# First eight attention steps without normalized weights: 1/sum is turned by TensorE and applied to the values

## The chip, the cores and the metric

The kernel runs on one core of a Trainium2 chip. The metric is the device time of one execution in microseconds; the kernel before was timed three times and the median counts. A core has five engines that each work through their own queue in program order: TensorE (PE) for matrix products and transposes, VectorE (DVE), ScalarE (ACT), GpSimd (POOL) and SyncE (SP), whose queue here issues nearly all DMAs. An instruction waits for semaphores that other instructions raise, and everything behind it on its engine waits with it.

## The reference

Attention over 8 sequences of 576 tokens with 8 heads of 64, in which only weights close to the largest survive, then an MLP with an ELU. All is float32.

```python
scores = scale * np.matmul(q, k.transpose(0, 1, 3, 2))
thresh = np.max(scores, axis=-1, keepdims=True) - tau
scores = np.where(scores >= thresh, scores, -1000000000.0)
scores = scores - np.max(scores, axis=-1, keepdims=True)
attn = np.exp(scores)
attn = attn / (np.sum(attn, axis=-1, keepdims=True) + 1e-09)
return np.matmul(attn, v).astype(np.float32)
...
h = x @ w_in
g = np.where(h > 0.0, h, alpha * (np.exp(np.minimum(h, 0.0)) - 1.0))
return (g @ w_out).astype(np.float32)
```

The division by the row's sum can be done on the weights, before the product with v, or on the product, since the sum belongs to a row of queries.

## The kernel before

Heads are taken two at a time: a pair `pr` is one sequence's heads 2j and 2j+1, four pairs to a sequence. A pair has five steps `i`: four blocks of 128 queries, and one (`NC`) with the last 64 queries of both heads. `steps` (L1175, L1176) lists them; for the first sequence the order is (0,0), (0,1), (1,0), (1,1), (2,0), (2,1), (3,0), (3,1), and then steps 2, 3 and NC of each pair. The numbers 0 to 7 in the task names are these first eight steps, and they make the first half (`part` 0, 256 queries) of the values of pairs 0 to 3.

A step goes through these functions, each an instruction or a few:

- `scores` (L657): PE forms 128 x 576 scores for each of the two heads in PSUM.
- `max_of` (L728, DVE), `bound_of` (L732, POOL) or `pivot_of` (L742, DVE): the row's largest score and the threshold.
- `exp_of` and `mask_of` (L761, L771): ACT makes the exponential, DVE keeps those above the threshold and adds up the row. Or `sink_of` and `raise_of` (L750, L756), where ACT does both. `mask_of` reads the scores in PSUM and frees their banks for a later step's `scores`.
- `total_of` (L778) and `reciprocal_of` (L785): DVE forms the sum and, at L789, its reciprocal `rs`, 128 x 2: one number for each query and head.
- a normalization for each head, which multiplies 128 x 576 weights by `rs`: on POOL (`normalize`, L722, instruction at L726), DVE (`normalize_dve`, L706, L709) or ACT (`normalize_act`, L711, L714). Which, is listed by hand in `ACT_NORM` and `NORM_DVE`; POOL has the rest.
- `turn_parts` (L803): PE turns the weights, 128 x 128 at a time (`transpose`, L791), into `rt` in PSUM, and ACT or DVE copies them into `wTa` or `wTb` (L808).
- `values` (L915): when a part's steps are turned, PE multiplies with v, one product with `vd` (L925) and eight with `vm` (L930), into `pv` in PSUM.
- `values_out` (L1055): ACT copies `pv` into `xt`, the MLP's input (L1060).

In the early phase `rt` and `pv` share two PSUM buffers. `room_for` keeps a queue of them: whoever wants a third first lets the oldest be read out.

The order of the instructions on all engines in this phase is made by `early_tasks` (L1308). Each `task` has a due time, a correction by hand from the table `MOVED`, and the tasks that it needs. The tasks are taken by due time, and `do` (L1299) first does what a task needs. A task that nothing pulls forward stands where its due time puts it; a large due time means that it is done just when something needs it. So the due times fix a program order and nothing else; on the chip an instruction runs when it is at the head of its queue and its semaphores are up.

Around the change:

- The queries of pair 0 come in two pieces. The first 256 are loaded at the start. The rest are loaded by `load_rest_of_q` (L1337) into the buffer `qr`, 128 x 320, of which there is one, and turned by DVE in `rest_of_q` (L1342); they are needed from the ninth step, (0,2), on.
- SP issues loads in program order (L544 for q and k, L558 and L560 for v, L478 for pieces of the MLP's weights, `wst`). In the stretch that matters here, the order is: k and q of a later pair, the four DMAs of `qr`, one `wst`, v of pair 3, v of pair 2, then more `wst`. v of a pair is two `vm` and two `vd`.
- The weights of the MLP come in a form that POOL, ACT and DVE convert between the attention's instructions (`convert_rest` L485, `convert_shift` L492 and L494, `convert_add` L500, `convert_rest_pool` L505, `convert_abs` L510, `convert_end` L518).
- The MLP's first product, `ffn1` (L1091, PE at L1102), starts when all four pairs' `xt` exist.

Of the kernel before, what the change touches and what calls it, by code (L numbers as in the profile page):

```python
# [10 lines left out]
FP32 = mybir.dt.float32  # L11
# [4 lines left out]
ALU = mybir.AluOpType  # L16
# [352 lines left out]
def kernel(  # L369
# [10 lines left out]
    nc = tc.nc  # L380
    PSUM = bass.MemoryType.PSUM
    P = 128
    B, H, S, D = q.shape
# [5 lines left out]
    T = 32  # L389
    NT = P // T  # L390
# [3 lines left out]
    NPAIR = H // 2  # L394
# [22 lines left out]
    wstage = early.enter_context(tc.tile_pool(name="wstage", bufs=2))  # L417
    wpool = [wstage]
    banks = ExitStack()
    psum = {"t": banks.enter_context(tc.tile_pool(name="ps_t", bufs=2, space=PSUM))}  # L420
# [214 lines left out]
    wTs, xts, open_steps, turns = {}, {}, {}, {}  # L635
# [142 lines left out]
    def total_of(pr, i, hs):  # L778
        st = open_steps[pr, i]
        cs = slice(hs[0], hs[-1] + 1)  # L780
        if "summed" not in st:
            st["summed"] = True
            nc.vector.tensor_reduce(st["su"][:, cs], st["sm"][:, cs], axis=AX.X, op=ALU.add)

    def reciprocal_of(pr, i, hs):  # L785
        st = open_steps[pr, i]
        cs = slice(hs[0], hs[-1] + 1)
        total_of(pr, i, hs)
        nc.vector.reciprocal(st["rs"][:, cs], st["su"][:, cs])  # L789

    def transpose(dst, src):  # L791
        nc.tensor.matmul(dst, src, idents[-1], is_transpose=True, skip_group_check=True)  # L792
# [104 lines left out]
    def fetch(pr, i):  # L897
        back = turns.pop((pr, i)).rearrange("c k p n -> (c k) p n")
        wT, g0 = turned_tile(pr, i)
        if i < NC:  # L900
            nc.sync.dma_start(wT[:, g0 : g0 + NT].rearrange("p g c n -> p g (c n)"), back)
        elif pr >= JOINED:
            for h in range(2):
                g = h * (3 * NT - 2)
                nc.sync.dma_start(
                    wT[:, g : g + 2, h * NC : h * NC + NC + 1].rearrange("p g c n -> p g (c n)"),
                    back[:, 2 * h : 2 * h + 2],
                )
        else:
            nc.sync.dma_start(  # L910
                wT.rearrange("p (a b) c n -> p a b (c n)", b=2)[:, ::5],
                back.rearrange("k (a b) n -> k a b n", b=2),
            )

    def values(pr, part, pv=None):  # L915
        b, j = divmod(pr, NPAIR)
# [138 lines left out]
    def values_out(pr, part, pv):  # L1055
        b, j = divmod(pr, NPAIR)
        q0, n = TAIL * part, (3 if part else 2) * NT * T
        watch = on_banks if wide else lambda *a: None
        o = pv[:, q0 : q0 + 2 * P]
        watch(nc.scalar.copy(xts[b][:, j, part * 2 * P : (part + 1) * 2 * P], o), o)  # L1060
        if part:
            xs = opool.tile([P, TAIL], FP32, name="xs", bufs=2)
            for h in range(2):
                r = slice(h * D, (h + 1) * D)
                o = pv[r, h * (n - TAIL) : h * (n - TAIL) + TAIL]
                watch(nc.scalar.copy(xs[r], o), o)  # L1066
            nc.sync.dma_start(xtail[j, :, b * TAIL : (b + 1) * TAIL], xs)
            pairs.pop(pr), raws.pop(pr)
# [106 lines left out]
    steps = [(pr, i) for pr in range(NP) for i in ((0, 1, NC, 2, 3) if pr >= JOINED else range(NB))]  # L1175
    steps[:per_seq] = [(pr, i) for x in ((0, 1), (2, 3, NC)) for pr in range(NPAIR) for i in x]  # L1176
    LATE = 10

    def behind(pr, i):
        if i in (1, NB - 1):  # L1180
# [114 lines left out]
    def task(x, t, key, f, *needed):  # L1295
        each = "_".join(map(str, x)) if isinstance(x, tuple) else x
        made[x] = [t + (MOVED.get(key, 0.0) if key else 0.0) + MOVED.get(each, 0.0), len(made), f, needed, False]

    def do(x):  # L1299
        job = made[x]  # L1300
        if not job[4]:
            job[4] = True
            for y in job[3]:
                if y:
                    do(y)
            job[2]()

    def early_tasks():  # L1308
# [5 lines left out]
        def room_for(pool, release):  # L1314
            while len(taken[pool]) >= 2:
                taken[pool].popleft()()
            taken[pool].append(release)
# [54 lines left out]
        for pr in range(1, NPAIR + 6):  # L1372
            old = ("sc", number[pr - 2, NC]) if pr > 1 else None
            own = pr < NPAIR
            for x, name in enumerate("qk"):
                n = 2 * pr - 2 + x if own else number[pr - 1, 2 + x]
                k, late_ = kind(n), n >= LATE
# [26 lines left out]
                m = number[pr, 2] if own and not x else n  # L1404
# [15 lines left out]
        for i, (n, x) in enumerate(slots):  # L1420
            late_, k, t = n >= LATE, f"{kind(n)}{x}", begin[n]
            m, y = slots[max(i - 4, 0)]
# [47 lines left out]
        for n in range(MIDDLE):  # L1470
            pr, i = steps[n]
# [4 lines left out]
            t, k, hs, late_ = begin[n], kind(n), heads_of(i), n >= LATE  # L1476
# [10 lines left out]
            for h in hs:  # L1487
                task(("max", n, h), at_(0.2 + 0.5 * h, 1.8 + 0.6 * h, 0.8 + 0.5 * h), f"max{h}{k}", lambda pr=pr, i=i, h=h: max_of(pr, i, h), ("sc", n))
                back = ("turned", n - (2 if last_ else WBUFS)) if n >= WBUFS else None
                t_exp, t_th, t_mask = (at_(0.3 + 0.7 * h, 2.0 + 0.6 * h, 1.0 + 0.5 * h), at_(0.4 + 0.7 * h, 2.2 + 0.6 * h, 1.1 + 0.5 * h),  # L1490
                                       at_(2.0 + 1.6 * h, 5.6 + 0.1 * h, 4.0 + 0.1 * h))
                if (n, h) in MASK_ACT:
                    task(("exp", n, h), t_exp, f"exp{h}{k}", lambda pr=pr, i=i, h=h: sink_of(pr, i, h), ("th", n, h), back, "late" if last_ else None)
                    task(("th", n, h), t_th, f"th{h}{k}", lambda pr=pr, i=i, h=h: pivot_of(pr, i, h), ("max", n, h))
                    task(("mask", n, h), t_mask, f"mask{h}{k}", lambda pr=pr, i=i, h=h: raise_of(pr, i, h), ("exp", n, h))
                else:
                    task(("exp", n, h), t_exp, f"exp{h}{k}", lambda pr=pr, i=i, h=h: exp_of(pr, i, h),
                         ("max", n, h), exps[-1] if exps else None, ("mask", *exps[-2][1:]) if len(exps) > 1 else None)
                    task(("th", n, h), t_th, f"th{h}{k}", lambda pr=pr, i=i, h=h: bound_of(pr, i, h), ("max", n, h))
                    exps.append(("exp", n, h))  # L1500
                    task(("mask", n, h), t_mask, f"mask{h}{k}", lambda pr=pr, i=i, h=h: mask_of(pr, i, h), ("exp", n, h), ("th", n, h),
                         ("mask", n, 0) if h and (n, 0) not in MASK_ACT else back, "late" if last_ else None)
                scaled = normalize_act if (n, h) in ACT_NORM else normalize_dve if (n, h) in NORM_DVE else normalize_pool
                norm = lambda pr=pr, i=i, h=h, f=scaled: f(pr, i, h)
                task(("norm", n, h), at_(5.0 + 0.8 * h, 6.2 + 0.1 * h, 5.4 + 0.1 * h), f"norm{h}{k}", norm, ("rec", n))
            task(("su", n), at_(3.8, 5.8, 4.4), f"su{k}", lambda pr=pr, i=i, hs=hs, f=total_act if n in SU_ACT else total_of: f(pr, i, hs), *[("mask", n, h) for h in hs])
            task(("rec", n), at_(3.8, 5.8, 4.4), f"rec{k}", lambda pr=pr, i=i, hs=hs: reciprocal_of(pr, i, hs), ("su", n))
            norms, part = [("norm", n, h) for h in hs], int(i >= 2)
# [9 lines left out]
            else:  # L1518
# [11 lines left out]
                m = n + 1  # L1530
# [14 lines left out]
            if i in (1, NC) and n < MIDDLE - 4:  # L1545
                got = []
                mine_ = [number[pr, x] for x in ((0, 1) if i == 1 else (2, 3, NC))]

                def run_values(pr=pr, part=part, got=got):
                    room_for("t", lambda: do(("out", pr, part)))  # L1550
                    got.append(values(pr, part))

                def run_out(pr=pr, part=part, got=got):
                    got[0]()
                    if (pr, part) == (NPAIR - 1, 0):
                        push_ffn(0)
                    elif (pr, part) == (NPAIR - 1, 1):
                        push_ffn(1)

                m = n + 2  # L1560
                t_val, t_out = (begin[m] + 4.0, begin[m] + 6.2) if m < LATE else (begin[m] + 0.4, begin[m] + 3.3)
                if n < per_seq:
                    t_val, t_out = begin[n + 1] + 4.2, begin[n + 2] + 1.5
                    if n >= LATE:
                        t_val, t_out = begin[n + 1] + 5.6, begin[n + 1] + 6.8
                elif any(m in SQUARES for m in mine_):
                    t_val, t_out = begin[n + 3] + 5.7, begin[n + 3] + 5.8
                elif SWITCH + 1 >= m >= SWITCH:
                    t_val, t_out = t_val - 8.0, t_out - 8.0
                task(("val", pr, part), t_val, f"val{k}", run_values, *[("landed", m) for m in mine_], ("v", pr))  # L1570
                task(("out", pr, part), t_out, f"out{k}", run_out, ("val", pr, part), ("out", pr, 0) if part else None)
            if n == 0:
                task("idle", t + 2.1, None, lambda: idle(16))
            if n >= SWITCH:
# [40 lines left out]
    with tc.manual_schedule():  # L1615
# [471 lines left out]
        for pr in range(JOINED, NP + 2):  # L2087
            t = clock[0]
# [263 lines left out]
```

## Time and profile before

| | us |
|---|---|
| median of three runs | 1258.88 (1258.06 to 1259.68) |
| profiled execution | 1259.32 |
| its span, first to last instruction | 1257.5 |
| PE busy | 1243.9 |
| DVE busy | 1040.3 |
| POOL busy | 727.1 |
| ACT busy | 635.2 |

A row of the time line has start, duration, engine, source line, operation, output and input with the tile's size, the number of instructions that it merges, and in brackets how long the engine was idle before and what ended that. "SPq" is SyncE's queue issuing a DMA. A row of the chain of waits has start, length, and the engine, tile and line. A row of groups has line, engine, operation, names, shapes and count, then busy us and the mean ns of one, then idle time ahead of the group. The table by stretches lists for each stretch the busy us and, in brackets, the instructions of each engine, then the granted clock and the DMA share.

### The profile page before, as it was taken

Reading aid. Unit: us, or ns where it says so; the run is one execution under the profiler, and the core shown is the slowest. Engines: PE = TensorE matmul, PEld = TensorE weight load, DVE = VectorE, ACT = ScalarE, POOL = GpSimd, SP = SyncE. Lnnn points to the kernel's source line nnn. Section 1 sums busy time; section 2 is a strip of 40 time slices with the busy share of each in tenths; the row PEclk is TensorE's granted clock in tenths of the full one; section 3 lists DMA queues with packets and bytes.
Section 4 is the critical chain, followed back from the end, with each engine's and each line's share of the span. In section 5 each row is a group of like instructions: output and inputs, shape, how many; then the busy total and the mean of one; then the engine's idle time right before and its main releaser. Section 6 shows DMA issues by size and latency. Waiting matters only on the chain.

```text
span 1257.5 us, 21116 instructions
## 1 busy us (share of the span) xinstructions
PE 1243.9 (99%) x6598; PEld 957.0 (76%) x6598; DVE 1040.3 (83%) x2199; ACT 635.2 (51%) x1331; POOL 727.1 (58%) x1061
## 2 busy tenths in 40 slices
PE   8999999999999999999999999999999999999998
PEld 6676576467878787888778787878788887788886
DVE  7888778789798988898889879898889876776983
ACT  7989776664352526253534435252625353465330
POOL 4778655687475847666576747584766655122000
PEclk9999999999999999999999999999999999999999
DMA  7557688998889898998989998999889885000001
GB/s 134 151 177 177 177 244 234 260 248 216 239 239 266 245 240 224 241 263 228 252 206 253 237 231 231 256 257 240 228 238 262 221 241 175 20 1 1 1 34 34
DMA packets 325551, 245.74 MB, mean 195 GB/s; under 512 B 209216, under 2 KB 289984, under 8 KB 325440
## 3 DMA queue, kind: packets, MB, share of 16 engines
q1 hardware_dynamic: 323264, 243.65, 72.2%
q8 instruction: 52, 0.85, 0.3%
q10 hardware_dynamic: 2176, 0.75, 0.2%
q14 instruction: 59, 0.48, 0.1%
HBM read 154.53 MB, written 89.78 MB: 194 GB/s over the span
## 4 chain that ended last, share of the span: by engine, by line
PE 90%; DVE 3%; DMA 2%; ACT 2%; issue 1%; SPq 1%; POOL 1%; DVEq 0%; ACTq 0%; POOLq 0%
PE f L1678 23%; PE f L1818 22%; PE sc L977 8%; PE sc L1050 7%; PE f L2278 7%; PE f L2203 5%; PE f L1102 4%; PE sc L673 3%; PE f L1154 3%; PE f L2216 2%; PE pv L930 2%; PE rt L792 1%; PE sc L1042 1%; PE sc L1037 1%; DMA there<-x 1%
## 5 line engine op out<-in xcount | busy, mean ns | idle before, releaser
L984 DVE TENSOR_REDUCE mx<-sc 128x1 f32<-128x576 f32 x207 | 148.3, 750 | 28.5 <-PE sc L977 24.6
L726 POOL TENSOR_SCALAR w<-w,rs 128x576 f32<-128x576 f32 x144 | 115.8, 813 | 70.0 <-DVE rs L789 69.8
L1004 ACT ACTIVATE w<-sc,mx 128x576 f32<-128x576 f32 x113 | 81.5, 740 | 116.0 <-DVE mx L984 98.7
L868 DVE STREAM_TRANSPOSE x<-w 128x512 f32<-128x512 f32 (+1 forms) x153 | 108.9, 744 | 15.3 <-POOL w L726 11.3
L996 POOL TENSOR_SCALAR th<-mx,ntau 128x2 f32<-128x2 f32 (+1 forms) x114 | 33.8, 297 | 133.3 <-DVE mx L984 133.3
L977 PE MATMUL sc<-kT,qT 64*128 64x448 f32 (+4 forms) x736 | 103.4, 416 | 0.2 <-ACT xs L1066 0.2
L977 PEld LDWEIGHTS sc<-kT,qT 64*128 64x128 f32 x736 | 81.0, 186 | 25.1 <-issue 16.5
L1011 DVE SCALAR_TENSOR_TENSOR w<-sc,th,w 128x576 f32<-128x576 f32 x113 | 88.2, 811 | 9.4 <-ACT w L1004 9.2
L1678 PE MATMUL f<-xt,sw 128*128 128x256 f32 x384 | 93.8, 386 | 1.8 <-DVE g L1700 1.8
L1678 PE MATMUL f<-xt,w_in 128*128 128x256 f32 x384 | 92.2, 382 | 0.0
L1818 PE MATMUL f<-w_out,s 128*128 128x256 f32 x384 | 92.0, 382 | 0.1
L1818 PE MATMUL f<-w_out,g 128*128 128x256 f32 x384 | 92.0, 382 | 0.0
L1678 PE MATMUL f<-x,w_in 128*128 128x256 f32 x384 | 90.9, 379 | 0.0
L1818 PE MATMUL f<-t,s 128*128 128x256 f32 x384 | 90.8, 379 | 0.0
L726 POOL TENSOR_SCALAR e<-e,rs 128x576 f32<-128x576 f32 x91 | 67.1, 741 | 35.6 <-DVE rs L789 34.2
L1678 PEld LDWEIGHTS f<-xt,sw 128*128 128x128 f32 x384 | 69.4, 189 | 18.6 <-issue 4.8
L1678 PEld LDWEIGHTS f<-xt,w_in 128*128 128x128 f32 x384 | 71.7, 190 | 12.7 <-ACT w L1692 2.2
L1818 PEld LDWEIGHTS f<-w_out,g 128*128 128x128 f32 x384 | 72.0, 190 | 12.4 <-issue 3.1
L1818 PEld LDWEIGHTS f<-w_out,s 128*128 128x128 f32 x384 | 71.9, 190 | 12.4 <-issue 2.5
L1678 PEld LDWEIGHTS f<-x,w_in 128*128 128x128 f32 x384 | 72.8, 190 | 10.5 <-ACT s L1692 0.6
L1818 PEld LDWEIGHTS f<-t,s 128*128 128x128 f32 x384 | 72.8, 190 | 10.3 <-POOL s L1765 0.4
L1765 POOL TENSOR_TENSOR s<-g 128x256 f32<-128x256 f32 x96 | 74.9, 785 | 7.9 <-DVE g L1728 7.5
(316 smaller groups left out, 3103.5 us busy)
## 6 DMA issues: line engine op xcount, KB each, us to landing
there<-x SPq DMA_DIRECT2D x444, 144.0 KB, 3.5
wTb<-there SPq DMA_DIRECT2D x58, 576.0 KB, 6.5
wTa<-there SPq DMA_DIRECT2D x53, 576.0 KB, 5.0
sw<-win_sums SPq DMA_DIRECT2D x46, 384.0 KB, 4.9
t<-wout_sums SPq DMA_DIRECT2D x33, 512.0 KB, 6.2
qm<-in_q_dram SPq DMA_DIRECT2D x124, 72.0 KB, 4.9
wst<-in_moe_w_in_dram SPq DMA_DIRECT2D x16, 512.0 KB, 4.4
vm<-in_v_dram SPq DMA_DIRECT2D x64, 128.0 KB, 3.9
```

The source lines that it names most:

```text
L726: nc.gpsimd.tensor_scalar(wv, wv, st["rs"][:, h : h + 1], 1.0, ALU.mult, ALU.mult)
L868: nc.vector.transpose(x[:, :, c0 : c0 + nc_], src.rearrange("p (c g n) -> p g c n", c=nc_, n=T))
L977: on_banks(nc.tensor.matmul(o, qT[r, i * P : (i + 1) * P], kT[r, k0 : k0 + n], start=True, stop=True, skip_group_check=True), o)
L984: on_banks(nc.vector.tensor_reduce(st["mx"][:, h : h + 1], st["sc", h], axis=AX.XY if i == NC else AX.X, op=ALU.max, negate=True), st["sc" ...
L1004: on_banks(nc.scalar.activation(st["e", h], st["sc", h], AF.Exp, bias=st["mx"][:, h : h + 1]), st["sc", h])
L1011: on_banks(nc.vector.scalar_tensor_tensor(st["e", h], st["sc", h], st["th"][:, h : h + 1], st["e", h], ALU.is_ge, ALU.mult, accum_out=st[" ...
L1050: on_banks(nc.tensor.matmul(o, vm[:, h, c], parts[part][:, g0:g1, h * (NC + 1) + c], start=False, stop=(c == NC - 1), skip_group_check=Tru ...
L1678: nc.tensor.matmul(loc["banks"][place], left[:, j], right[:, j], start=(begins and j == 0), stop=(j == 1), skip_group_check=True)
L1765: engine.tensor_tensor(o, x, y, op)
L1818: nc.tensor.matmul(place(m), lhs, rhs, start=(begins and v == 0), stop=(v == RU - 1), skip_group_check=True)
L2203: nc.tensor.matmul(o, w.rearrange("p (j f) -> p j f", j=KJ)[:, j], m, start=(j == 0 and x == 0), stop=(j == KJ - 1 and x == 1), skip_group ...
L2278: nc.tensor.matmul(banks8[2 * i + x // 2], h[:, tok], w, start=(f == 0 and x != 1), stop=(f == NFT - 1 and x != 0), skip_group_check=True)
```

## The change

Part 0 of pairs 0 to 3 is `UNSCALED`: `(0,0)`, `(1,0)`, `(2,0)`, `(3,0)` as (pair, part).

- The normalizations of the first eight steps (16 in all) are not done.
- For these steps the reciprocal writes 128 x 128 instead of 128 x 2: each head's number is written 64 times beside itself, into one of three buffers `rsd`.
- Ahead of the values of such a part, PE turns the two steps' `rsd` into one `rt` buffer (`spread`): row h*64+d, column query holds 1/sum of that query for head h, which is the layout of `pv`.
- ACT copies these 256 columns into SBUF (`keep_spread`). The room for this is the buffer `qr`, the same one that the rest of pair 0's queries is loaded into.
- DVE multiplies `pv` by it into `xt`, in place of ACT's copy.
- The new tasks have a due time of 9000, so they stand right before the first that needs them. In program order the kept scales of pairs 0 and 1 come before the load of `qr`, those of pairs 2 and 3 behind its use.

```diff
+        if (pr, int(i >= 2)) in UNSCALED:
+            st["rs"] = wstage.tile([P, 2, D], FP32, name="rsd", bufs=3)
+            nc.vector.reciprocal(st["rs"], st["su"].unsqueeze(2).broadcast_to([P, 2, D]))
+            return
         nc.vector.reciprocal(st["rs"][:, cs], st["su"][:, cs])
...
+    scales = {}
+
+    def spread(pr):
+        rt = psum["t"].tile([P, 512], FP32, name="rt", tag="rt")
+        for i in range(2):
+            transpose(rt[:, i * P : (i + 1) * P], open_steps[pr, i]["rs"].rearrange("p h d -> p (h d)"))
+        return rt
+
+    def keep_spread(pr, rt):
+        room = wstage.tile([P, S // T - 2 * NT, T], FP32, name="qr", bufs=1).rearrange("p j d -> p (j d)")
+        scales[pr] = room[:, : 2 * P]
+        nc.scalar.copy(scales[pr], rt[:, : 2 * P])
...
-        watch(nc.scalar.copy(xts[b][:, j, part * 2 * P : (part + 1) * 2 * P], o), o)
+        if (pr, part) in UNSCALED:
+            nc.vector.tensor_tensor(xts[b][:, j, : 2 * P], o, scales.pop(pr), ALU.mult)
+        else:
+            watch(nc.scalar.copy(xts[b][:, j, part * 2 * P : (part + 1) * 2 * P], o), o)
...
+    UNSCALED, LAST = [(pr, 0) for pr in range(NPAIR)], 9000.0
...
+                if (pr, int(i >= 2)) in UNSCALED:
+                    norm = lambda: None
...
+                    def run_spread(pr=pr, got_spread=got_spread):
+                        room_for("t", lambda: do(("scales", pr)))
+                        got_spread.append(spread(pr))
+
+                    task(("spread", pr), LAST, None, run_spread, *[("rec", m) for m in mine_])
+                    task(("scales", pr), LAST, None, lambda pr=pr, got_spread=got_spread: keep_spread(pr, got_spread[0]),
+                         ("spread", pr), ("out", pr - 1, 0) if pr else None)
-                task(("val", pr, part), t_val, f"val{k}", run_values, *[("landed", m) for m in mine_], ("v", pr))
-                task(("out", pr, part), t_out, f"out{k}", run_out, ("val", pr, part), ("out", pr, 0) if part else None)
+                task(("val", pr, part), t_val, f"val{k}", run_values, *[("landed", m) for m in mine_], ("v", pr),
+                     ("spread", pr) if (pr, part) in UNSCALED else None)
+                task(("out", pr, part), t_out, f"out{k}", run_out, ("val", pr, part),
+                     ("out", pr, 0) if part else ("scales", pr) if (pr, 0) in UNSCALED else None)
```

On the queues this gives: on SP the same DMAs in the same order, but the first of `qr` now waits until DVE's multiplication for pair 1 has read the buffer. On DVE that multiplication stands right behind a `convert_end` (L518) of the seventh step; the multiplication for pair 3 stands between the `pivot_of` (L748) and the `convert_shift` (L494) and `mask_of` (L775) of the tenth step. On PE the two transposes of `rsd` stand right ahead of each part's values.

More of the change, by code (lines that the diff above doesn't have):

```diff
@@ L1569, in early_tasks @@
                     t_val, t_out = t_val - 8.0, t_out - 8.0
-                task(("val", pr, part), t_val, f"val{k}", run_values, *[("landed", m) for m in mine_], ("v", pr))
-                task(("out", pr, part), t_out, f"out{k}", run_out, ("val", pr, part), ("out", pr, 0) if part else None)
+                if (pr, part) in UNSCALED:
+                    got_spread = []
+                    def run_spread(pr=pr, got_spread=got_spread):
[8 more added lines that the diff above has]
+                     ("out", pr, 0) if part else ("scales", pr) if (pr, 0) in UNSCALED else None)
             if n == 0:
```

## The prediction, as it was put on record

> **What bounds the kernel now.** The page's head and the table by stretches come first.
>
> ```profile
> span 1257.5 us, 21116 instructions
> PE 1243.9 (99%) x6598; PEld 957.0 (76%) x6598; DVE 1040.3 (83%) x2199; ACT 635.2 (51%) x1331; POOL 727.1 (58%) x1061
> ...
> 0.00:62.40 62.40, 55.80 (x344) 40.04 (x344) 47.95 (x113) 50.61 (x98) 38.60 (x70) 1.00 0.62 143
> 62.40:1257.50 1195.10, 1188.11 (x6254) 916.95 (x6254) 992.34 (x2087) 584.60 (x1234) 688.49 (x992) 1.00 0.73 198
> ...
> 12.00:36.00 24.00, 21.66 (x147) 14.45 (x145) 20.54 (x48) 21.48 (x42) 15.62 (x27) 1.00 0.81 169
> ...
> 37.90:62.40 24.50, 23.41 (x143) 16.89 (x141) 20.01 (x44) 22.72 (x45) 19.78 (x26) 1.00 0.42 132
> ```
>
> The columns behind the comma are PE, PEld, DVE, ACT and POOL. From 62.4 us on PE is idle for 1195.1 - 1188.1 = 7.0 us in all, so whatever the first 62 us gain or lose reaches the end nearly whole. The change touches only those, and there no engine is full. What sets the pace there stands in the chain of waits:
>
> ```profile
> 12.63 1.33 POOL w L726 x2
> ...
> 14.07 0.75 POOL x L584
> ...
> 28.30 0.53 DVE w L709
> ...
> 37.98 0.63 PE pv L925 x2
> 38.60 1.88 PE pv L930 x16
> 40.48 1.32 PE sc L673 x8
> ...
> 62.41 0.41 PE rt L792 x2
> ```
>
> Two things are to be seen. Of the sixteen normalizations that go, only those at 12.63 and 28.30 are on the chain. And pair 2's values (37.98, 38.60) are on it: who delays them delays the run.
>
> **The change part by part.**
>
> *Gain.* At 12.63, 1.33 us leave the chain, but its next link, POOL's scaling at 14.07, needs queries that DVE turns until 12.47 + 0.78 = 13.25; so I take 14.07 - 13.25 = 0.8 of it. At 28.30 all 0.53 leaves. Together 1.3 us, and 1.9 at most. The others ran beside other work.
>
> ```profile
> 12.47 0.78 DVE L577 STREAM_TRANSPOSE x<-qm 128x576 f32<-128x576 f32 x1
> ```
>
> *Reciprocals.* The trace has no wide one. Its nearest rows:
>
> ```profile
> L789 DVE RECIPROCAL rs<-su 128x2 f32<-128x2 f32 x128 | 21.1, 165 | 10.0 <-ACT su L720 6.1
> ...
> L789 DVE RECIPROCAL rs<-su 128x1 f32<-128x1 f32 x32 | 5.2, 163 | 3.7 <-ACT su L720 2.8
> ...
> L808 DVE COPY wTb<-rt 128x128 f32<-128x128 f32 x4 | 1.1, 272 | 0.0
> ...
> L1700 DVE TENSOR_TENSOR g<-f,t 128x256 f32<-128x256 f32 x48 | 20.3, 422 | 1.6
> ```
>
> The second element costs 2 ns, so 128 come to 163 + 127 x 2 = 417 ns; a copy of as many takes 272. Between these I take 0.36 us, 0.19 over the narrow form. Six of them (steps 0 to 5) stand ahead of the place that decides: 1.2 us of DVE work (0.6 to 1.5). A multiplication of 128 x 256 is priced like the product out of PSUM in the last row, 0.42. So DVE has 1.2 + 0.42 - 0.53 = 1.1 us more to do up to there, against a gain of 1.3 on the chain: even. I keep early DVE times as they are, with 1.3 us to either side.
>
> *The load of `qr`.* This is the main term. It must now wait for pair 1's multiplication, and SP issues in order.
>
> ```profile
> 27.21 2.00 SPq L544 DMA_DIRECT2D qr<-in_q_dram  x4
> 29.26 0.46 SPq L478 DMA_DIRECT2D wst<-in_moe_w_in_dram  x1
> ...
> 33.18 0.59 SPq L558 DMA_DIRECT2D vm<-in_v_dram  x1
> 33.81 0.51 SPq L560 DMA_DIRECT2D vd<-in_v_dram  x1
> ```
> ```profile
> vd<-in_v_dram SPq DMA_DIRECT2D x1, 16.0 KB, 2.5
> ```
> ```profile
> 35.03 0.69 DVE L518 SCALAR_TENSOR_TENSOR w_in<-wtop,wst 128x512 f32<-128x512 f32 x1
> ...
> 37.29 0.51 DVE L1342 STREAM_TRANSPOSE x<-qr 128x320 f32<-128x320 f32 x1
> ```
> ```profile
> 29.95 1.95 PE L930 MATMUL pv<-wTb,vm 128*64 128x256 f32 x16
> ...
> 37.91 0.70 PE L925 MATMUL pv<-wTa,vd 128*128 128x256 f32 x2
> ```
>
> The multiplication stands behind L518, which ends at 35.03 + 0.69 = 35.7; it ends at 36.1, and `qr`, issued at 27.21 before, goes out at 36.2: 9.0 us late. Queued behind it are one `wst`, the v of pair 3 and the v of pair 2. The last `vd` of pair 2 was issued at 33.81 and took 2.5 us to land, 36.3; pair 2's values began at 37.91, so 1.6 us were spare. Now it lands at 36.3 + 9.0 = 45.3 and the values begin at 45.4: 7.5 us late (6.2 to 8.8). PE works in order, so all its later work stands behind.
>
> Two other engines are held by the same load. DVE's turning of `qr` at 37.29 waits till about 36.2 + 2.0 + 1.9 = 40.1, and ACT's conversion of the late `wst` (37.06 below) till it has landed, 29.26 + 4.4 + 9.0 = 42.7 at the soonest:
>
> ```profile
> qr<-in_q_dram SPq DMA_DIRECT2D x1, 40.0 KB, 1.9
> ...
> wst<-in_moe_w_in_dram SPq DMA_DIRECT2D x1, 512.0 KB, 4.4
> ```
> ```profile
> 37.06 0.68 ACT L510 ACTIVATE wst<-wst 128x512 int32<-128x512 f32 x1
> ```
>
> Both are shorter than 7.5 us and lie under it, but they leave neither engine free to run ahead. Where the stall goes: it isn't taken up again, as between 37.9 and 62.4 PE had only 24.5 - 23.4 = 1.1 us idle.
>
> *Pair 3's multiplication.* It is put ahead of L494 and L775 on DVE and waits for the values:
>
> ```profile
> 47.92 1.95 PE L930 MATMUL pv<-wTb,vm 128*64 128x256 f32 x16
> ...
> 50.44 1.21 PE L673 MATMUL sc<-x,qd 128*128 128x288 f32 x4
> ```
> ```profile
> 48.95 0.42 DVE L494 TENSOR_SCALAR wtop<-wst 128x512 uint32<-128x512 uint32 x1
> 49.46 0.82 DVE L775 SCALAR_TENSOR_TENSOR w<-sc,th,e 128x576 f32<-128x576 f32 x1
> ```
>
> In the times of before: the values end at 47.92 + 1.95 = 49.87, two transposes later 50.1; the multiplication ends at 50.5, L494 at 50.9, and the mask starts 1.4 us behind 49.46. The scores of 50.44 wait for that mask's PSUM banks. I take 1.0 us (0.5 to 1.5), as PE's wait at 62.4 gives some back.
>
> *The remaining edits cost nothing.* The first six transposes of `rsd` run while PE waits for v or for ACT; uncovered they would be a tenth of a microsecond each. ACT's copies of the scales take the place of its copies of `pv`, of the same size.
>
> *PE's clock.* While it waits for v, PE stands still for 45.4 - 38.1, some 7 us. What does it run at then?
>
> ```profile
> 1.48 4.66 PE L792 MATMUL rt<-ident 128*128 128x128 f32 x22 [1.48 <-POOL ident masks.py:199]
> ...
> 9.56 1.23 PE L673 MATMUL sc<-x 64*128 64x288 f32 x4 [1.12 <-ACT w L753]
> 10.72 1.97 PE L792 MATMUL rt<-ident 128*128 128x128 f32 x16
> ```
>
> The first 22 transposes took 0.21 us each, 16 later ones 0.12, these soon after a pause of 1.12 us. No row has a pause of 7 us. If it works like a start, pair 2's values (37.91 to 40.4, 2.5 us) take 0.21/0.12 as long, 1.9 us more; if like the short pause, nothing. A pause that long is nearer to the start; since some of the stretch waits for other engines anyway I take 1.4.
>
> [...]
>
> *Sum.* 7.5 + 1.0 + 1.4 = 9.9 us, to the profiled execution's own 1259.32, which is 0.44 above the median: 1269.2, or 1268.8 beside the median. Ends: 6.2 + 0.5 + 0 = 6.7 and 8.8 + 1.5 + 1.9 = 12.2, so 1265.6 to 1271.1.
>
> **The rivals.**
>
> *Each element of a reciprocal costs what the first does.* A small operation on one element beside it:
>
> ```profile
> L436 DVE TENSOR_SCALAR keep<-pos 128x1 f32<-128x1 f32 x1 | 0.2, 154 | 0.1
> ```
>
> The reciprocal of one element takes 163 - 154 = 9 ns more. If each of 128 pays about that, one takes 0.154 + 128 x 0.009 = 1.3 us, 1.14 more than before; six are 6.8 us ahead of pair 1's multiplication. DVE was idle for 24.0 - 20.5 = 3.5 us between 12 and 36, which takes up part, not all, since the chains behind grow as well: 4.8 us on the end, 1273.6. Against it: the second element costs 2 ns. For it: two elements are few, and a floor under small sizes would hide it. [...]
>
> *The delay is partly taken up.* If ACT, POOL and DVE, rid of sixteen normalizations, run ahead behind 42 us, PE makes up its 1.1 us of idle time, and the early end holds: 6.2 - 1.1, 1264.0. Against it: of the normalizations still on the chain there, none goes.
>
> *Not slower.* If the multiplication for pair 1 is over by 27.21 + 1.6 = 28.8, pair 2's v comes in time, and what is left is the gain: 1258.9 - 1.3 = 1257.6. That is the point that decides. Against it: the multiplication needs pair 1's values, which end at 29.95 + 1.95 = 31.9, and no normalization of 1.3 us moves these by more than 3 us.
>
> **How the numbers follow.** The forecast as put, 1265.6 to 1271.1: 0.52. Slow reciprocals: 0.34. Partly taken up: 0.10. Not slower: 0.04, of which 0.03 is faster. Changes below 0.2% (2.5 us) can't be told from none here. The predicted time is that of the forecast, 1268.8. The range goes from 1264 to 1275, the one end for the delay partly taken up, the other for slow reciprocals with all their other terms at full. Faster 0.03, within 0.2% 0.02, slower 0.95.
>
> **What would show it.** SP's issue of `qr` at about 36 instead of 27 us, with its wait named for DVE; PE's row of pair 2's first product at about 45, idle some 7 us before it and released by a DMA of v; the transposes or products right behind at nearly twice their time; the mean of the wide reciprocal, under 0.45 us or over 1; the stretch from pair 3's values to the first MLP products about 1 us longer. If `qr` goes out before 30 us, the main term falls; if it does go late and pair 2's values don't start late, the order of the v loads was read wrongly.

## The result, and the profile after

The changed kernel takes 1272.26 us (median of four runs, 1271.29 to 1273.45); beside it the kernel before took 1258.47. The ratio is 1.0108, 95% interval 1.0095 to 1.0121: 13.6 us slower by the ratio, 13.8 by the two medians. The forecast was 1268.8. The profiled execution took 1271.29, with a span of 1269.5, 12.0 longer than before; it is the shortest of its four, and that of before lay above its median, so the spans show less than the medians.

The head of the page of after, and the table by stretches (columns as before), first for before from its first MLP product on, then for after:

```profile
span 1269.5 us, 21115 instructions
...
PE 1247.2 (98%) x6606; PEld 958.4 (75%) x6606; DVE 1047.3 (83%) x2202; ACT 633.0 (50%) x1327; POOL 720.0 (57%) x1050
```
```profile
51.48:1257.50 1206.02, 1198.52 (x6313) 925.41 (x6311) 1002.23 (x2104) 594.61 (x1254) 697.88 (x1002) 1.00 0.73 198
```
```profile
64.51:1269.50 1204.99, 1198.46 (x6313) 925.25 (x6311) 1002.32 (x2104) 593.80 (x1252) 699.04 (x1002) 1.00 0.73 198
40.00:45.00 5.00, 0.43 (x4) 0.19 (x2) 2.99 (x6) 0.00 (x0) 0.07 (x1) 0.91 0.83 199
45.00:50.00 5.00, 2.66 (x10) 1.48 (x12) 0.98 (x3) 3.60 (x7) 3.11 (x4) 0.50 0.83 234
50.00:55.00 5.00, 5.00 (x36) 3.17 (x34) 2.59 (x6) 1.61 (x3) 0.66 (x1) 0.91 0.05 20
```

From the first MLP product on PE was idle for 1206.02 - 1198.52 = 7.5 us before and is for 1204.99 - 1198.46 = 6.5 us after, with the same 6313 instructions and the same busy time. So of the 13.0 us by which that product comes late, 1.0 is made up behind it, and 12.0 reach the end. Most of the loss lies in one hole, 40 to 50 us, where PE did 3.1 us of work in 10; from 45 to 50 us PE had a granted clock of 0.50.

The time line of after, SP's queue, then PE, then DVE, then POOL and ACT:

```profile
38.10 1.82 SPq L544 DMA_DIRECT2D qr<-in_q_dram  x4
...
44.81 0.47 SPq L560 DMA_DIRECT2D vd<-in_v_dram  x1
```
```profile
39.99 0.44 PE L796 MATMUL rt<-ident,rsd 128*128 128x128 f32 x2
47.34 1.19 PE L942 MATMUL pv<-wTa,vd 128*128 128x256 f32 x2 [6.91 <-ACT e L768]
48.46 3.14 PE L947 MATMUL pv<-wTa,vm 128*64 128x256 f32 x16
...
59.22 0.62 PE L942 MATMUL pv<-wTb,vd 128*128 128x256 f32 x2
...
63.47 1.21 PE L673 MATMUL sc<-x,qd 128*128 128x288 f32 x4 [1.17 <-DVE w L775]
64.51 1.89 PE L1122 MATMUL f<-xt,w_in 128*128 128x256 f32 x8
```
```profile
37.62 0.42 DVE L1078 TENSOR_TENSOR xt<-pv,qr 128x256 f32<-128x256 f32 x1
...
41.59 0.51 DVE L1363 STREAM_TRANSPOSE x<-qr 128x320 f32<-128x320 f32 x1 [2.08 <-DMA qr<-in_q_dram]
...
54.98 0.94 DVE L791 RECIPROCAL rsd<-su 128x128 f32<-128x128 f32 x1
...
61.83 0.42 DVE L1078 TENSOR_TENSOR xt<-pv,qr 128x256 f32<-128x256 f32 x1 [0.94 <-PE pv L947]
62.17 0.42 DVE L494 TENSOR_SCALAR wtop<-wst 128x512 uint32<-128x512 uint32 x1
62.50 0.81 DVE L775 SCALAR_TENSOR_TENSOR w<-sc,th,e 128x576 f32<-128x576 f32 x1
```
```profile
44.93 1.04 POOL L492 TENSOR_TENSOR wtop<-wst,eight 128x512 int32<-128x512 int32 x1 [7.09 <-DMA wst<-in_moe_w_in_dram]
```
```profile
47.19 0.73 ACT L753 ACTIVATE w<-sc,th 128x576 f32<-128x576 f32 x1
```

What SP's queue waited for (total us, times, longest), and the groups of the two new operations:

```profile
SPq L544 <- DVE xt L1078: 9.8, 1, 9.8
```
```profile
L791 DVE RECIPROCAL rsd<-su 128x128 f32<-128x128 f32 x8 | 7.6, 952 | 0.6 <-ACT su L720 0.4
L1078 DVE TENSOR_TENSOR xt<-pv,qr 128x256 f32<-128x256 f32 x4 | 1.7, 421 | 3.6 <-PE pv L947 3.6
```

Pair 1's multiplication ends at 38.04 and SP, which stood 9.8 us for it, issues `qr` at 38.10. The last `vd` of pair 2 goes out at 44.81 and takes 2.4 us to land in this trace, so it is there at 47.2; pair 2's values start at 47.34. The row names ACT's exponential as the releaser, but that only happened to end at nearly the same moment, 46.56 + 0.72 = 47.28. With v loaded first (below) the same product starts 6 us ahead of that exponential. In the run with 44 transposes v comes later: there the exponential ends at 47.51, the last `vd` goes out at 46.05, and the product starts at 48.56, again 2.5 us behind the `vd`, and names it.

The shift against before, place by place: pair 2's values start 47.34 - 37.91 = 9.4 late, pair 3's 59.22 - 47.29 = 11.9, the scores behind them 63.47 - 50.44 = 13.0, the first MLP product 64.51 - 51.48 = 13.0. And a wide reciprocal took 0.95 us, not 0.36.

### The profile page after: what moved, and what is told of

Same layout as the page of the kernel before. It is cut to its first block, busy times and chain, and to the rows that moved or that the text cites. A ratio compares the mean times of both kernels' runs of the same rounds, so it can differ in the third digit from the quotient of the medians.

```text
span 1269.5 us, 21115 instructions
## 1 busy us (share of the span) xinstructions
PE 1247.2 (98%) x6606; PEld 958.4 (75%) x6606; DVE 1047.3 (83%) x2202; ACT 633.0 (50%) x1327; POOL 720.0 (57%) x1050
## 4 chain that ended last, share of the span: by engine, by line
PE 90%; DVE 4%; DMA 2%; ACT 1%; issue 1%; SPq 1%; POOL 0%; DVEq 0%; ACTq 0%; POOLq 0%
PE f L1853 23%; PE f L1713 22%; PE sc L994 8%; PE sc L1067 7%; PE f L2313 7%; PE f L2238 5%; PE f L1122 5%; PE sc L673 3%; PE f L1174 3%; PE f L2251 2%; PE pv L947 2%; PE rt L796 2%; PE sc L1059 1%; DMA there<-x 1%; PE sc L1054 1%
## 5 line engine op out<-in xcount | busy, mean ns | idle before, releaser
L726 POOL TENSOR_SCALAR w<-w,rs 128x576 f32<-128x576 f32 x133 | 107.5, 818 | 62.7 <-DVE rs L793 62.4
```

Source lines behind the costliest of these rows:

```text
L726: nc.gpsimd.tensor_scalar(wv, wv, st["rs"][:, h : h + 1], 1.0, ALU.mult, ALU.mult)
```

## The experiments

Times are against the kernel before on the same chip (medians 1258.5 to 1259.2); the ratio's interval in us is in brackets. "First product" is the start of the first MLP product in the profile, against 51.48 before, in one profiled execution each.

| run | time over before, us | first product, us |
|---|---|---|
| the change | +13.6 (12.0 to 15.2) | +13.0 |
| scales apart from `qr` | +4.8 (3.0 to 6.4) | +5.0 |
| two-wide reciprocals, spread by GpSimd | +10.4 (8.8 to 12.2) | +11.2 |
| two-wide reciprocals, spread by VectorE | +10.1 (8.2 to 12.1) | +11.1 |
| both edits (scales apart, GpSimd) | +2.0 (0.9 to 3.1) | +2.2 |
| both, pair 3 alone unscaled | +2.0 (0.9 to 3.1) | +1.5 |
| both, pairs 0 to 2 alone unscaled | +1.5 (0.4 to 2.6) | +0.5 |
| before with wide reciprocals alone | +6.4 (4.8 to 8.2) | +5.6 |
| v ahead of `qr` | +8.3 (6.5 to 10.1) | +10.4 |
| 44 extra transposes in the pause | +13.6 (11.6 to 15.5) | +14.1 |
| 60 extra transposes in the pause | +11.5 (9.7 to 13.2) | +11.5 |

### Scales apart from `qr`

```diff
-        room = wstage.tile([P, S // T - 2 * NT, T], FP32, name="qr", bufs=1).rearrange("p j d -> p (j d)")
-        scales[pr] = room[:, : 2 * P]
+        b, j = divmod(pr, NPAIR)
+        if b not in xts:
+            xts[b] = xpool.tile([P, KJ, MAIN], FP32, name="xt")
+        scales[pr] = xts[b][:, j, 2 * P :]
```

> The changed kernel with one edit: the spread scales lie in the half of xt that is written later, not in the buffer that the load of qr fills. Nothing else moves, nothing computed changes. Theory: the cost of 13.8 us has three parts, the late load of qr with the slow PE clock behind it (about 7), the wide reciprocals of 0.95 us (about 5 to 6), pair 3's multiplication ahead of the mask (about 1.2). By it qr goes out near 27 us again, pair 2's values start 5 to 6.5 us later than before instead of 9.4, no 5 us stretch behind 40 us has a granted clock under 0.8, and the time is before + 7 (5.5 to 8.5). Rival 'the load is all': before + 1 to 2.5. Rival 'the reciprocals are all, the load is hidden under them': before + 11 to 13.8, as the changed kernel.

1263.40 us, +4.8. The time line of this kernel:

```profile
28.52 2.00 SPq L544 DMA_DIRECT2D qr<-in_q_dram  x4
...
40.23 0.60 PE L944 MATMUL pv<-wTa,vd 128*128 128x256 f32 x2
...
51.22 0.62 PE L944 MATMUL pv<-wTb,vd 128*128 128x256 f32 x2
...
56.52 1.89 PE L1124 MATMUL f<-xt,w_in 128*128 128x256 f32 x8
```

`qr` is back where it was, but for 1.3 us, and the hole and the low clock are gone (granted 1.00 from 45 to 50 us). The shared buffer costs 13.6 - 4.8 = 8.8 us, more than the 7 expected, and what is left, 4.8, is less than the expected 5.5 to 8.5: pair 2's values are 2.3 late, where 5 to 6.5 had been expected, probably because a wide reciprocal holds DVE, but no weights wait for it any more (see the wide reciprocals alone, below). Both rivals lie outside the interval.

### Two-wide reciprocals, spread by GpSimd, then by VectorE

```diff
-            st["rs"] = wstage.tile([P, 2, D], FP32, name="rsd", bufs=3)
-            nc.vector.reciprocal(st["rs"], st["su"].unsqueeze(2).broadcast_to([P, 2, D]))
+            nc.vector.reciprocal(st["rs"][:, cs], st["su"][:, cs])
+            rs, st["rs"] = st["rs"], wstage.tile([P, 2, D], FP32, name="rsd", bufs=3)
+            nc.gpsimd.tensor_copy(st["rs"], rs.unsqueeze(2).broadcast_to([P, 2, D]))
```

> The changed kernel with one edit: VectorE takes the reciprocal of two sums a row, as before the change, and GpSimd copies it out to 128 x 128. The scales still lie in the buffer of qr. Theory of three parts: qr goes out at 35.5 to 36.5 instead of 38.1, pair 2's values start 7 to 8.5 us later than before, the granted clock behind 45 us is near 0.5 again, the time is before + 9.5 (8 to 11). Rival 'the load is all': before + 12 to 13.8. Rival 'the reciprocals are all': before + 1 to 2.5.

1269.51 us, +10.4, as the theory expected; the second rival falls, the first lies at the interval's upper edge. `qr` goes out at 36.0 and pair 2's values start at 45.14, 7.2 late. The second run has `nc.vector.tensor_copy` in the last line:

> The changed kernel with one edit: VectorE takes the reciprocal of two sums a row and spreads it itself by a copy, 0.166 + 0.222 = 0.39 us in place of 0.95, near the 0.36 that the forecast took for a wide reciprocal. All else of the change stays, the shared buffer of qr too. Theory that only the size of this term was off: what the forecast's sum gives, before + 9.9 (9.5 to 11.5), qr issued at 36.2 to 37.2, pair 2's values at 45 to 46. Rival 'other terms were off as well and cancelled': outside before + 8.5 to 12.5.

1268.83 us, +10.1. On its time line the steps of the forecast come out one after the other:

```profile
36.35 1.86 SPq L544 DMA_DIRECT2D qr<-in_q_dram  x4
...
45.58 1.19 PE L943 MATMUL pv<-wTa,vd 128*128 128x256 f32 x2 [6.87 <-ACT e L768]
```

The forecast had 36.2 for the issue and 45.4 for the values. So with a spread reciprocal near the price that the sum assumed, the sum holds in time, 10.1 against 9.9, and up to pair 2's values step by step. Behind these it holds only roughly: the profiled execution, the longest of its four, has its first MLP product 11.1 us late, of which the low clock took 2.0 on pair 2's values instead of the 1.4 assumed. The reciprocals were the term that was badly mis-sized.

### Both edits together

> Both edits together: scales in the unused half of xt, and reciprocals of two sums a row copied out by GpSimd. Theory of three parts: what is left is pair 3's multiplication ahead of the mask, before + 1.5 (0.5 to 2.5), the first MLP products 1 to 2 us later than before, and up to 45 us no more than 0.5 us of delay. A rival, 'a part is missing' (the transposes of the scales or ACT's copies cost time by themselves): over before + 3, with the delay already there at pair 2's values. A rival on the other side, 'the gain of the removed normalizations shows once the two costs are gone': below before - 0.5.

1261.38 us in the median of eleven, +2.0: two edits take back 11.6 of the 13.6 us. Neither rival is borne out by the median: no gain shows, and 2.0 is left. The profiled run was the longest of the eleven, with a low clock early on (the last section); its pair 2's values, 0.9 us late, are over the 0.5 expected, and the low clock fits that: in the run with pairs 0 to 2 alone, which has the same edits for these pairs and not the low clock, they are 0.2 us late.

### Pair 3 alone, and pairs 0 to 2 alone

Both have the two edits above. In the first:

```diff
-    UNSCALED, LAST = [(pr, 0) for pr in range(NPAIR)], 9000.0
+    UNSCALED, LAST = [(NPAIR - 1, 0)], 9000.0
```

> The changed kernel with pair 3 alone unscaled (pairs 0 to 2 normalized as before the change), scales in the unused half of xt, reciprocals of two sums a row copied out by GpSimd: pair 3's multiplication ahead of the mask by itself. Theory: the first MLP products 1.1 us later than before (0.8 to 1.6), all of it behind pair 3's values, time before + 1.2 (0.4 to 2). Rival 'the freed normalizations of pair 3 pay for it': within 0.4 of before. Rival 'what is left with both edits, 2.0 us, is not this multiplication but the first pairs': the same, within 0.4 of before.

In the second, `range(NPAIR - 1)`:

> Both edits (scales in the unused half of xt, reciprocals of two sums a row copied out by GpSimd), and pair 3 normalized as before the change, so that pairs 0 to 2 alone are unscaled. Theory: the change without its three costs is even, within 0.8 of before, and over 1 us under the kernel with both edits alone; up to pair 3's values it stands where that one did. Rival 'the twelve normalizations that go are worth something': before - 1 to - 2. Rival 'the first three pairs cost too': before + 1 or more.

1261.36 us, +2.0, and 1260.03 us, +1.5. The first kept to its expectation at the upper edge; the second missed, being not within 0.8 and not clearly under the kernel with both edits. Its median meets the rival that the first three pairs cost too (1 or more), though the interval reaches down to 0.4. The traces see more than the times here. From pair 3's first product to the scores that wait for the mask, it takes 3.15 us before (47.29 to 50.44), 4.25 in the change, 4.23 with pair 3 alone (47.65 to 51.88), and 3.12 with pairs 0 to 2 alone (47.83 to 50.95): the multiplication ahead of the mask costs 1.1 us, and it is there exactly where pair 3 is unscaled. But its 1.1 us and the rest of pairs 0 to 2 don't add up to the times at this resolution, and which part of the last 2 us lies where stays open. No version tried is faster than the kernel before.

### Wide reciprocals alone, in the kernel before

```diff
+        if n_of(pr, i) < 8:
+            st["rs"] = wstage.tile([P, 2, D], FP32, name="rsd", bufs=3)
+            nc.vector.reciprocal(st["rs"], st["su"].unsqueeze(2).broadcast_to([P, 2, D]))
+            st["rs"] = st["rs"][:, :, 0]
+            return
```

> The kernel before with one edit: in the first eight steps the reciprocal is taken of 128 x 128 spread sums instead of 128 x 2, and the normalizations read one column a head. Nothing else of the change is in it. It prices the wide reciprocals alone. Theory of three parts: mean of one 0.93 to 0.98 us, and before + 6 (4 to 7), as DVE has 8 x 0.79 = 6.3 us more work and nearly no room. Rival 'DVE's idle time of 3.5 us between 12 and 36 us takes up the most': before + 0 to 3. The load of qr goes out near 27 us in either case.

1264.97 us, +6.4, the mean of one 952 ns. By the medians the same eight instructions cost twice as much here as in the change (13.6 - 10.4 = 3.2). An explanation that fits, but was not tested by itself: before, each stands between a sum and the weights that wait to be normalized, so its length lies on the chain; in the change only pairs' values wait for it.

### The price by size

The kernel before, with the reciprocals of the first six steps taken of 128 x 4 up to 128 x 128, and in steps 6 and 7 a copy and then a reciprocal of 128 x 128 without a broadcast read:

> The kernel before with the reciprocals of the first six steps taken of 128 x 4, 8, 16, 32, 64 and 128 (each sum spread by a broadcast read), and in steps 6 and 7 a copy that spreads the sums to 128 x 128 and a reciprocal of that copy without a broadcast. What is asked is the mean of each size, the time is before + 2 to 5. 'A fixed part and a rate': (952 - 165)/126 = 6.25 ns an element from the second on, so 178, 203, 253, 353, 553 and 952 ns. 'As cheap as other work up to some size, dear above it': under 200 ns up to 16 elements. 'The broadcast read makes it dear': the reciprocal of the copy takes under 0.5 us instead of 0.95, and the copy itself is dear.

One run, 1263.21 us, 4.0 over before. Its groups on VectorE, the mean ns of one behind the comma:

```profile
L799 DVE RECIPROCAL rsd<-rsd 128x128 f32<-128x128 f32 x2 | 1.9, 954 | 0.1
...
L794 DVE RECIPROCAL rsd<-su 128x128 f32<-128x128 f32 x1 | 1.0, 954 | 0.0
L794 DVE RECIPROCAL rsd<-su 128x64 f32<-128x64 f32 x1 | 0.6, 554 | 0.0
L797 DVE COPY rsd<-su 128x128 f32<-128x128 f32 x2 | 0.4, 222 | 0.0
L794 DVE RECIPROCAL rsd<-su 128x32 f32<-128x32 f32 x1 | 0.4, 355 | 0.4 <-ACT su L720 0.4
L802 DVE RECIPROCAL rs<-su 128x2 f32<-128x2 f32 x2 | 0.3, 166 | 0.1
L794 DVE RECIPROCAL rsd<-su 128x16 f32<-128x16 f32 x1 | 0.3, 253 | 0.0
L794 DVE RECIPROCAL rsd<-su 128x8 f32<-128x8 f32 x1 | 0.2, 203 | 0.0
L794 DVE RECIPROCAL rsd<-su 128x4 f32<-128x4 f32 x1 | 0.2, 178 | 0.0
L802 DVE RECIPROCAL rs<-su 128x1 f32<-128x1 f32 x1 | 0.2, 164 | 0.0
```

From two elements on the sizes lie on a line, 154 + 6.25 n ns: 179 for 4, 204 for 8, 254, 354, 554 and 954 for 128. The broadcast read has no part in it: the reciprocal of a plain tile takes 954 as well, and the copy that does the spreading 222. Only the row for one element, 164 where the line has 160, lies off it, and the step from one element to two is 2 ns for that reason.

### v ahead of `qr`

```diff
-        task("loadr", -97.0, None, load_rest_of_q, "start")
+        task("loadr", -97.0, None, load_rest_of_q, "start", ("v", 3), ("v", 2))
```

> The changed kernel with the v of pairs 3 and 2 issued on SP ahead of qr instead of behind it; qr and one wst still wait for pair 1's multiplication. Theory as in the prediction, that of all that stands behind qr only pair 2's v sets the delay and the turning of qr lies under it: v lands in time, the next to be late is the turning of qr on VectorE at about 41.6, which holds the scores and masks behind it for some 4 us instead of the pause of 6.9. So before + 11 (9 to 12), no pause of PE over 5 us ahead of pair 2's values, which start near 40 to 41. Rival 'qr itself was the late one and v only stood beside it': before + 13 to 13.8, with the pause as long but behind pair 2's values instead of ahead of them. Rival 'v alone was late, qr is needed by nobody so early': before + 4.8, the time with the scales apart.

1267.88 us, +8.3, under the expected 9 to 12. Pair 2's values start at 40.17 with no wait for v, so v was what held them; that rules out the first rival, and 8.3 against 4.8 rules out the second. The chain of waits shows what is late next:

```profile
39.38 3.26 DMA qr<-in_q_dram
...
43.35 0.95 DVE rsd L791
44.30 0.62 DVE mx L730
...
44.98 1.05 POOL wtop L492
...
46.62 0.72 ACT e L768
47.34 0.64 ACT w L753
...
48.02 2.29 PE sc L673 x6
```

POOL's conversion (L492), ACT's conversion of the same piece, its exponential and its next instruction on those weights (L753, of `sink_of`) follow one another, and PE waits 3.94 us for the last of them, up to 48.02. As what POOL waited for, the chain names DVE's maximum, behind the turning of `qr` and a wide reciprocal. But L492 reads only the `wst` and a constant, and the `wst` stands in SP's queue right behind `qr`: it was issued at 39.88, 5.1 us before POOL starts, and the same load took 4.8 us to land in the changed kernel, while the maximum only ended beside it, at 44.92. In the changed kernel POOL's row, shown above, names the `wst` itself, and the maxima had ended by 44.39, 0.5 us before. So the second delay is the late `wst`, not the turning of `qr` that was expected. In the changed kernel this second chain ends at 47.19 + 0.73 = 47.92, 0.6 us behind the start of pair 2's values, which PE does ahead of the scores that need it. The two delays lie side by side, so taking v's away alone wins back 5.3 of the 8.8 us in time, and in the profiles 2.6 of 8.0 at the first MLP product.

### Work in PE's pause

```diff
+        if (pr, part) == (2, 0):
+            for _ in range(44):
+                transpose(pv[:, :P], ident)
         watch(nc.tensor.matmul(pv[:, :n], vd, wT[:, :, NC], start=True, stop=False, skip_group_check=True), pv[:, :n])
```

> The changed kernel with 44 transposes of the identity put on TensorE directly ahead of pair 2's values, into the PSUM tile that the values then overwrite; they are extra work of about 44 x 0.12 = 5.3 us that lies in the pause before the late v lands. Theory that the pause itself halves the clock behind it: the granted clock is 1.0 between 45 and 50 us, pair 2's products take 0.6 and 1.95 us instead of 1.19 and 3.14, the values still start near 47.3, and the time falls by 1.8 us (1 to 2.5) from the changed kernel's, to before + 12 (11 to 13). Rival 'the clock is low for another reason, or the slow stretch is covered by other engines': the time stays at before + 13.5 within 0.7, or the transposes run at half rate themselves and it goes above before + 14.

1272.59 us, +13.6: no gain, yet no verdict either. One `vd` issue took 1.60 us, v came at 48.56, and 2.92 us of pause were left; the clock went to 0.50 all the same, 2.7 us into it. With `range(60)`:

> As the run with 44 extra transposes, but with 60, which at the 0.113 us each of that run take 6.8 us and end near 47.4, so that no pause over 1.2 us is left ahead of pair 2's values (with 44 there was still one of 2.92 us, and the granted clock fell 2.7 us into it). Theory that a pause of 2 to 4 us brings the clock down: it is 1.0 all through 40 to 55 us, pair 2's products take 0.6 and 1.95 us, the values start at 47.4 to 48.6 and end 1.0 to 1.8 us earlier against their start than in the changed kernel; time before + 11 to 12.8. Rival 'the slow clock costs nothing, as other engines are awaited behind it': the clock is 1.0, but the time stays at before + 13.5 within 0.7. Rival 'the clock falls for another reason': it is 0.5 behind 45 us again.

1270.22 us, +11.5. The time line and one stretch (granted clock third from the end):

```profile
40.48 6.71 PE L796 MATMUL pv<-ident 128*128 128x128 f32 x60
47.51 0.67 PE L945 MATMUL pv<-wTa,vd 128*128 128x256 f32 x2 [0.31 <-DMA vd<-in_v_dram]
48.11 1.95 PE L950 MATMUL pv<-wTa,vm 128*64 128x256 f32 x16
```
```profile
45.00:50.00 5.00, 4.69 (x41) 3.33 (x38) 2.71 (x7) 3.63 (x7) 3.21 (x4) 1.00 0.81 220
```

The values start 0.2 us later than in the change and take 0.67 and 1.95 us instead of 1.19 and 3.14. That shows that here the pause brought the clock down. With more work on PE the kernel is 2.1 us faster by the ratios and 1.5 at the first product, so the low clock costs some 1.5 to 2.1 us; the two intervals in time overlap, and the size rests on the profiles.

## Why the prediction was right, and where it was off

The direction, the place and the main mechanism held; the time came out 3.5 us above the forecast. It lies above the forecast's own ends, 1265.6 to 1271.1, and inside the range only because that was widened to 1275 for the rival of slow reciprocals, which is the term that failed.

- *The load of `qr`.* Right in each link: SP waits 9.8 us for pair 1's multiplication, v of pair 2 lands late, PE stands still for 6.9 us. 9.4 us late instead of 7.5, and nearly all of the 1.9 more comes from the reciprocals ahead of it: 7.7 without them (the copy on VectorE). "It isn't taken up again" held but for 1.0 us: that much of PE's idle time behind the first MLP product is gone, close to the 1.1 that the rival *The delay is partly taken up* reckoned with. "Both are shorter than 7.5 us and lie under it" was right in the outcome and wrong in a size: ACT's conversion of the late `wst` came at 46.01, 9.0 us late, not at 42.7, since the `wst` itself landed 2.1 us later than reckoned and POOL's L492, 1.04 us, stands between. It still lies under the values, as PE does these first: the chain's last link ends at 47.92, and PE reaches the scores behind it at 51.53.
- *PE's clock.* 1.4 was assumed; pair 2's values took 51.53 - 47.34 = 4.2 us instead of 2.5, so 1.7, and the run with 60 transposes gives 1.5 to 2.1. It came out near the upper end, 1.9, which was priced like the start. That the start is the same thing is not shown: its transposes were slow, 0.21 us each, but the profile's granted clock stands at 1.00 through the first 10 us of both kernels. Behind the pause it stood at 0.50 from 45 to 50 us, and in the run with 44 transposes a pause of 2.92 us was already long enough for that.
- *Pair 3's multiplication.* 1.0 assumed, 1.1 in the trace up to the scores. What PE's later waits give back, which the forecast had already taken off here, comes on top: the 1.0 us above.
- *The gain, and the multiplication on DVE.* The multiplication was 0.42 us as priced. Without the wide reciprocals, pair 1's values started at 29.12 to 29.57 in the three such runs that had no low clock ahead of them, against 29.42 before. So of the gain of 1.3 on the chain no more than 0.3 is left there; what takes up the rest wasn't tried. The change has nearly nothing to set against its costs.
- *Reciprocals: the term that failed.* "The second element costs 2 ns, so 128 come to 163 + 127 x 2 = 417 ns" took a rate from two rows that don't differ by the rate. It is 6.25 ns an element, 0.95 us each. That was worth 13.6 - 10.4 = 3.2 us, or 3.5 against the copy on VectorE, by which the forecast, 9.9, would have been 13.1 to 13.4. The rival *Each element of a reciprocal costs what the first does* had the kind right, and by its own reckoning (4.8 us for 1.14 more each) 0.79 more would come to 3.3; its 9 ns an element were too many. 128 elements took 954 ns, a copy of as many 222, so an element costs far more than in a copy, and a difference of 2 ns between two rows was too little to set against that rival.
- The count was short too: six wide reciprocals were counted, and that of step 7 stands behind pair 2's values (54.98) and ahead of pair 3's. There after loses another 11.9 - 9.4 - 1.7 = 0.8 us. Where the copy on VectorE takes its place the same stretch loses 0.3, so some 0.5 of it is the reciprocal's, and the rest stays open.

Laid end to end, these stretches of the trace make up the whole delay: 9.4 + 1.7 + 0.8 + 1.1 = 13.0 us at the first MLP product, and 12.0 at the end.

## What to carry to other kernels

Before a buffer is shared to save room, look at who writes it next and what is queued behind that write: here the scales themselves cost little (+2.0 us for the whole change once they had a place of their own and the reciprocals were two wide), and the DMA that had to wait 9.8 us for them held up the loads queued behind it, for somebody else. A rate per element isn't read from rows of one and two elements: here these took 164 and 166 ns, 2 ns apart, where the rate was 6.25 ns; a second size well above is needed, or the range must reach to the dear end. When one queue makes two things late by nearly as much, mending one wins back only a part, here 5.3 of 8.8 us: ask what ends right beside the wait that is named. And a named releaser is checked against what the instruction reads: twice here it was an instruction that only ended at the same moment as the load.

## What the runs showed of the hardware

- In the run with the sizes a reciprocal on VectorE took 154 ns and 6.25 ns an element from 2 to 128 elements a partition, and at 128 as long with a broadcast read as without, 954 ns; a copy of 128 x 128 took 222 ns.
- PE's granted clock fell to 0.50 at no one fixed time in these runs: 3.7 us into the pause of the change, 2.7 in the run with 44 transposes, 2.3 in the one with GpSimd's copy, 4.2 in the one with VectorE's copy, and 1.9 in the one with v ahead of `qr`, where a pause of 0.7 us stood shortly before. It came back 3.6, 3.2, 5.8, 4.2 and 4.8 us after work resumed. The mean clock of half a microsecond shows the edge, in the change and in the run with GpSimd's copy:

```profile
43.50:44.00 0.50, 0.00 (x0) 0.00 (x0) 0.50 (x2) 0.00 (x0) 0.00 (x0) 1.00 1.12 274
44.00:44.50 0.50, 0.00 (x0) 0.00 (x0) 0.47 (x2) 0.00 (x0) 0.00 (x0) 0.59 1.20 274
```
```profile
40.00:40.50 0.50, 0.00 (x0) 0.00 (x0) 0.47 (x4) 0.00 (x0) 0.00 (x0) 1.00 0.77 213
40.50:41.00 0.50, 0.00 (x0) 0.00 (x0) 0.50 (x2) 0.00 (x0) 0.00 (x0) 0.73 0.95 253
```

- In one run the clock fell without a long pause. In the profiled execution with both edits no pause of PE between 4 and 11 us was over 1.12 us, and the granted clock was 0.50 from 12 to 14:

```profile
10.00:12.00 2.00, 2.00 (x12) 1.56 (x12) 1.16 (x3) 2.00 (x6) 0.27 (x1) 0.79 0.86 151
12.00:14.00 2.00, 2.00 (x11) 2.00 (x10) 1.95 (x5) 1.93 (x4) 1.03 (x2) 0.50 1.01 293
```

Sixteen transposes took 3.21 us there instead of 1.97. In all the other profiled runs the granted clock was 1.00 from 10 to 14 us, and why it fell in this one stays open.
